# Sending a weight matrix's tail to chosen DMA engines through GpSimd's queue

## The chip, the cores and the metric

The kernel runs on one core of one Trainium2 chip. The metric is the time of one execution on the device in microseconds (us); lower is better. The page counts 16 DMA engines, and in the kernel before 16 packets are under way at 92 of 99 instants taken every 5 us (17 or 18 at the other seven). "The trace" is one profiled execution: every instruction, and for every DMA packet its start, its duration, its bytes and its queue. The trace does not say on which engine a packet ran. Engine numbers in this document are those that the marks of e3, e4 and e9 give; in the plan of the change they are what the author meant.

## The reference, cut to what matters

```python
x  = A_x                                    # 4 x 1 x 640, bf16
xn = layernorm(x)
# attention, 32 heads, head size 192, the last 2048 of 8192 cached keys
q  = xn @ wq
p  = softmax(q @ k.T * 192**-0.5)           # k, v: 2048 x 192 per head and batch
att = (p @ v) @ wo
# feed-forward: w1, w3 640 x 1536, w2 1536 x 640
ffn = (silu(xn @ w1) * (xn @ w3)) @ w2
out = x + att + ffn
```

Nearly all of the work is reading: 3 MB of K and 3 MB of V for each head, and the weights, 223 MB in all. w1 is under 2 MB of that.

## The kernel before: the parts that matter

Nearly all loads are issued by SyncE into one queue. A load of a tile of 128 partitions leaves 128 data packets in the trace, eight for each of the 16 engines, and 16 packets of 4 bytes, one for each engine. w1 has 640 rows of 1,536 numbers (3,072 bytes). 640 is five times 128, and the kernel splits it in three: 512 rows on all engines (four rows to a partition), 64 rows as 128 half rows on all engines, and 64 rows in small loads of 12 partitions (`w1_low`) on three engines alone. (The kernel before leaves 1,324 packets of 4 bytes on SyncE's queue. It has 82 loads of 128 partitions and four of 12, and 1,324 is 82 x 16 + 4 x 3.)

```python
LE, LI = 3, 4
LP, LF, LB = LE * LI, CT + LE * LI, KM * P + PH     # 12, 44, 576; CT = 32, KM = 4, PH = 64
FM, FH = KM * F, KM * F + F // 2

def w1_load():
    w = B_w1
    wt = fpool.tile([P, FH + F], BF16, tag="w", name="w1")
    we = wopool.tile([LF, 2 * F], BF16, tag="wo", name="w1e")
    nc.gpsimd.memset(we[:], 0.0)
    nc.gpsimd.memset(wt[0:LF, FH:], 0.0)
    nc.sync.dma_start(out=wt[:, 0:FM], in_=w[0:KM * P, :].rearrange("(p kc) n -> p (kc n)", kc=KM))
    nc.sync.dma_start(out=wt[:, FM:FH], in_=w[KM * P:LB, :].rearrange("r (h n) -> (r h) n", h=2))   # the half rows
    ...

def w1_low(n):                                      # called four times, between the loads of the heads
    if n < 2:
        b0 = LB + n * 2 * LP
        nc.sync.dma_start(out=we[n * CT:n * CT + LP, :],
                          in_=w[b0:b0 + 2 * LP, :].rearrange("(i e s) n -> e i (s n)", e=LE, s=2))
    ...

def w3_load():
    wt = fpool.tile([P, KC, F], BF16, tag="w", name="w3")
    nc.sync.dma_start(out=wt[:].rearrange("p k n -> p (k n)"), in_=B_w3.rearrange("(p kc) n -> p (kc n)", kc=KC))
```

The rest of the kernel loads K and V head by head, multiplies and sums on VectorE and TensorE, and adds the products of w1, w3, w2 and wo where their data has arrived.

## Time and profile before

| | before |
|---|---|
| time | 525.76 us (525.65 to 525.87, 3 runs; 525.68 over 6 with the later ones) |
| span of the profiled run | 523.8 us |
| TensorE, VectorE busy | 69%, 65% |
| share of the 16 DMA engines' span taken by SyncE's packets | 99.2% |
| last DMA packet ends | 520.48 us |

From the page of the kernel before: busy times; the DMA rows, whose 40 places are equal slices of the span (busy tenths, then GB/s); then the queues with packets, megabytes and their share of 16 engines' span.

```profile
span 523.8 us, 4820 instructions
PE 361.8 (69%) x2336; PEld 75.9 (14%) x1643; DVE 340.9 (65%) x413; ACT 55.8 (11%) x176; POOL 5.6 (1%) x12
...
DMA  9999999999999999999999999999999999999996
GB/s 389 422 443 425 433 431 432 428 433 432 430 435 428 437 418 446 424 437 426 434 434 429 432 434 429 435 427 435 425 437 434 427 437 431 430 434 425 441 418 275
...
q1 hardware_dynamic: 11868, 222.96, 99.2%
q8 instruction: 15, 0.25, 0.2%
```

The DMA engines are busy nine tenths or more in 39 of the 40 slices and the compute engines are not. So the kernel ends when the slowest of the 16 engines has moved its share. Queue 8 is the fetching of the program itself, 15 packets of 16 KB; it runs on the same engines (a SyncE packet of 24,576 bytes beside such a fetch takes 1.3 to 1.5 us instead of 0.91).

The end of the chain of waits of the kernel before (start, length, what):

```profile
465.17 24.49 DMA vt<-in_A_v_cache_dram
...
489.68 30.66 DMA w<-in_B_w_dram
...
520.38 0.76 PE acc L264 x8
521.13 0.47 DVE res L542
```

After the last landing only about 3.4 us follow. Two stretches of the run will be compared later. Here they are for the kernel before; the columns are the window, its length, the busy time and count of PE, PEld, DVE, ACT and POOL, TensorE's granted clock, the DMA share and GB/s.

```profile
26.00:39.00 13.00, 9.03 (x31) 0.30 (x3) 8.46 (x10) 1.56 (x3) 0.00 (x0) 0.74 0.99 425
39.00:53.00 14.00, 8.12 (x37) 0.80 (x8) 12.57 (x15) 2.19 (x5) 0.00 (x0) 0.98 1.01 432
53.00:66.00 13.00, 11.11 (x69) 2.00 (x45) 10.46 (x12) 1.39 (x5) 0.00 (x0) 0.89 1.02 436
```

GpSimd's clear of the tail's tile, and two issues on SyncE's queue, from the timelines of the kernel before (start, length, engine, line, operation):

```profile
9.07 2.65 POOL L390 MEMSET w1e<- 44x3072 bf16 x1
```

```profile
65.95 0.55 SPq L132 DMA_DIRECT2D vt<-in_A_v_cache_dram  x1
82.18 0.34 SPq L439 DMA_DIRECT2D w<-in_B_w_dram  x1
```

### The profile page before, as it was taken

The page shows a single profiled execution, that of the slowest core. Times are in us where ns is not written, and L with a number is a line of the kernel's source. Part 1 is how long each engine was busy: PE and PEld are TensorE (multiplying, and loading weights), DVE is VectorE, ACT ScalarE, POOL GpSimd, SP SyncE. Part 2 cuts the span into 40 slices and gives each one's busy share as a digit, 9 for nine tenths or more (in the row PEclk, how much of TensorE's full clock was granted, in tenths as well). Part 3 has the DMA queues.
Part 4 walks back from the last instruction along what each step waited for, and adds up shares of the span by engine and source line. Part 5 has one row for each costly group of instructions (what it writes and reads, how often), then busy time and mean ns, then how long its engine had stood idle before and what let it go on. Part 6 is the DMA issues. An engine that isn't in the chain of part 4 may idle for free.

```text
span 523.8 us, 4820 instructions
## 1 busy us (share of the span) xinstructions
PE 361.8 (69%) x2336; PEld 75.9 (14%) x1643; DVE 340.9 (65%) x413; ACT 55.8 (11%) x176; POOL 5.6 (1%) x12
## 2 busy tenths in 40 slices
PE   0965866887668776667547768586686876675685
PEld 0100111121111111111111111111111111111122
DVE  3268853687656767577646877466667766667671
ACT  2111111111001110101100111001101110011111
POOL 4000000000000000000000000000000000000000
PEclk9979886898878998789997988889878898889988
DMA  9999999999999999999999999999999999999996
GB/s 389 422 443 425 433 431 432 428 433 432 430 435 428 437 418 446 424 437 426 434 434 429 432 434 429 435 427 435 425 437 434 427 437 431 430 434 425 441 418 275
DMA packets 11904, 223.26 MB, mean 426 GB/s; under 512 B 1332, under 2 KB 1608, under 8 KB 3052
## 3 DMA queue, kind: packets, MB, share of 16 engines
q1 hardware_dynamic: 11868, 222.96, 99.2%
q8 instruction: 15, 0.25, 0.2%
q14 instruction: 5, 0.04, 0.0%
q10 hardware_dynamic: 16, 0.01, 0.0%
HBM read 222.96 MB, written 0.01 MB: 426 GB/s over the span
## 4 chain that ended last, share of the span: by engine, by line
DMA 60%; PE 20%; DVE 15%; ACT 3%; issue 1%; SPq 1%
DMA kt<-in_A_k_cache_dram 44%; PE ps L288 11%; DMA w<-in_B_w_dram 11%; DVE pr L277 10%; DMA vt<-in_A_v_cache_dram 5%; PE po L361 4%; PE qps L243 3%; DVE sc L296 2%; ACT ex L324 1%; DVE z L332 1%; DMA x_sb<-in_A_x_dram 1%; PE mt L318 1%; ACT L324 0%; ACT negm L321 0%; PE mt L305 0%
## 5 line engine op out<-in xcount | busy, mean ns | idle before, releaser
L288 PE MATMUL ps<-pr,idb 128*128 128x512 bf16 x768 | 214.7, 422 | 137.6 <-DVE pr L277 137.5
L277 DVE TENSOR_TENSOR pr<-kt,qbc 128x3072 bf16<-128x3072 bf16 x128 | 223.5, 1746 | 104.0 <-DMA kt<-in_A_k_cache_dram 104.0
L296 DVE TENSOR_REDUCE sc<-ps 128x16 f32<-128x512 f32 x128 | 87.1, 681 | 2.7 <-PE ps L288 2.6
L340 PE MATMUL o_ps<-vt,z 128*8 128x384 bf16 x1024 | 60.5, 380 | 0.2 <-DVE z L332 0.2
L361 PE MATMUL po<-o_sb,sel_w 128*32 128x192 f32 x128 | 49.2, 518 | 0.6 <-ACT o_sb L343 0.6
L340 PEld LDWEIGHTS <-z 128*8 128x8 bf16 x1024 | 26.2, 95 | 98.8 <-issue 89.2
L332 DVE TENSOR_TENSOR z<-ex,mask_b 128x256 bf16<-128x256 bf16 x32 | 13.5, 423 | 38.6 <-ACT ex L324 38.6
L343 ACT COPY o_sb<-o_ps 128x384 f32<-128x384 f32 x32 | 15.3, 478 | 196.9 <-PE o_ps L340 196.9
L313 ACT ACTIVATE gneg<-gmax 1x128 f32<-1x128 f32 x32 | 9.8, 308 | 162.8 <-DVE gmax L310 162.8
L305 PEld LDWEIGHTS mt<-idf,lmax 128*1 128x1 f32 x32 | 3.2, 101 | 127.5 <-issue 125.5
L361 PEld LDWEIGHTS po<-o_sb,sel_w 128*32 128x32 f32 x128 | 13.8, 130 | 29.4 <-issue 27.9
L288 PEld LDWEIGHTS <-idb 128*128 128x128 bf16 x124 | 12.0, 97 | 39.3 <-issue 32.8
L318 PEld LDWEIGHTS mt<-ones_ff,gneg 1*128 1x128 f32 x64 | 9.6, 186 | 47.1 <-issue 43.7
L243 PE MATMUL qps<-wt,xnT 128*128 128x512 bf16 x59 | 14.9, 412 | 0.1
L318 PE MATMUL mt<-ones_ff,gneg 1*128 1x1 f32 x64 | 12.3, 259 | 0.7 <-ACT gneg L313 0.7
L321 ACT COPY negm<-mt 128x1 f32<-128x1 f32 x32 | 5.1, 159 | 70.4 <-PE mt L318 70.4
L310 DVE TENSOR_REDUCE gmax<-mt 1x4 f32<-1x128 f32 x32 | 8.8, 274 | 5.8 <-PE mt L305 5.8
L348 PEld LDWEIGHTS po<-rsum,tot_w 128*32 128x32 f32 x64 | 4.4, 108 | 51.5 <-ACT ex L324 35.4
L249 DVE CAST qbc<-qps 128x512 bf16<-128x512 f32 x6 | 3.8, 684 | 11.7 <-PE qps L243 11.7
L324 ACT ACTIVATE ex<-sc,negm 128x64 bf16<-128x64 f32 x32 | 11.1, 348 | 1.0
L305 PE MATMUL mt<-idf,lmax 128*1 128x128 f32 x32 | 10.9, 340 | 0.0
L199 PE MATMUL xnT_ps<-idb,xn 4*128 4x4 bf16 x5 | 0.4, 178 | 13.4 <-DVE xn L194 13.4
(74 smaller groups left out, 84.4 us busy)
## 6 DMA issues: line engine op xcount, KB each, us to landing
kt<-in_A_k_cache_dram SPq DMA_DIRECT2D x32, 3072.0 KB, 19.1
vt<-in_A_v_cache_dram SPq DMA_DIRECT2D x32, 3072.0 KB, 25.5
wo_t<-in_A_wo_dram SPq DMA_DIRECT2D x8, 960.0 KB, 20.7
wt<-in_A_wq_dram SPq DMA_DIRECT2D x2, 3072.0 KB
w<-in_B_w_dram SPq DMA_DIRECT2D x1, 1920.0 KB
wt<-in_A_wq_dram SPq DMA_DIRECT2D x1, 1536.0 KB, 19.5
w<-in_B_w_dram SPq DMA_DIRECT2D x1, 1536.0 KB
w<-in_B_w_dram SPq DMA_DIRECT2D x2, 640.0 KB
```

The source lines that it names most:

```text
L243: nc.tensor.matmul(qp[:], lhsT=xnT[:, kc].rearrange("p a b -> p (a b)"), rhs=wq_rows[kc][:, (c0 + i) * QC:(c0 + i + 1) * QC], start=(kc == ...
L277: nc.vector.tensor_tensor(out=pr[:], in0=kts[h][:, g * JQ:(g + 1) * JQ, :], in1=qbc[:, h * Dh:(h + 1) * Dh].unsqueeze(1).to_broadcast([P, ...
L288: nc.tensor.matmul(ps[:], lhsT=idb[:], rhs=pr[:, :, kk * DD:(kk + 1) * DD], start=(kk == 0), stop=(kk == NK - 1))
L296: nc.vector.tensor_reduce(out=scs[h][:, g * JQ:(g + 1) * JQ], in_=pss.pop(u)[:], axis=AX.X, op=ALU.add)
L305: nc.tensor.transpose(out=mt[0:1, 0:P], in_=chs[h][0][:], identity=idf[:])
L313: nc.scalar.activation(out=gneg[:], in_=gmax[:].unsqueeze(1).to_broadcast([1, PB, B]), func=ACTF.Copy, scale=-SCALE)
L318: nc.tensor.matmul(mt[:, P:P + 1], lhsT=gneg[:].rearrange("o p b -> o (p b)"), rhs=ones_ff[:], start=True, stop=True)
L324: nc.scalar.activation(out=ex[:], in_=scs.pop(h)[:], func=ACTF.Exp, bias=negm[:, 0:1], scale=SCALE, accum_out=rsum[:])
L332: nc.vector.tensor_tensor(out=z[:], in0=ex[:].unsqueeze(2).to_broadcast([P, NJ, B]), in1=mask_b[:].unsqueeze(1).to_broadcast([P, NJ, B]), ...
L340: nc.tensor.matmul(o_ps[c * CT:c * CT + 2 * B, :], lhsT=z[:, 2 * jj:2 * jj + 2, :], rhs=vt[:, 2 * jj:2 * jj + 2, :], start=(jj < 4), stop= ...
L343: nc.scalar.copy(out=o_sb[:], in_=o_ps[:])
L361: nc.tensor.matmul(po[sl, 0:Dh], lhsT=sel_w[:, par].rearrange("p a b -> p (a b)"), rhs=o_sb[:, par * Dh:(par + 1) * Dh].rearrange("p (r i) ...
```

## The change

Its intent is balance. The 64 rows that travelled as half rows over all 16 engines are to ride on engines that finish early. The place from which GpSimd's queue starts its next load is called the cursor here. That it starts where its last load ended was the author's assumption when the prediction was made; the loads of the tail show it later (by the marks on engines 0 and 1, then 2 and 3 in e4; on 4 and 5, then 7 and 8 in e9). So 24 rows go to one pair of engines and 40 to another, and three tiny loads into unused tiles (`skip`) stand between, to move the cursor by 4, 1 and 7. The widths 4, 2, 1, 2, 7 add up to 16; as planned, the pairs would be engines 4 and 5, and 7 and 8. The tail of w1 moves into one buffer of the value pool, w3 is loaded in two pieces, and eight more small matmuls take the tail.

24 rows go to partitions 16 to 23, 40 rows to partitions 60 to 67.

The diff, cut to its core (the operands of the tail are rebuilt to the new row order, which is left out, as are the matmuls and the new places of the small SyncE loads of `w1_low`):

```diff
-    KM, PH, LE, LI = KC - 1, P // 2, 3, 4
-    LP, LF, LB = LE * LI, CT + LE * LI, KM * P + PH
+    KM, LE, LI, SA, SB, GP = KC - 1, 3, 4, 3, 5, 8
+    LP, LF, LB = LE * LI, 68, KM * P
+    PA, PZ = 16, LF - GP
+    RA = LB + 5 * LP + LI
+    RB = RA + SA * GP
 ...
+    def skip(k):
+        t = const.tile([k, CT], BF16, name=f"skip{k}")
+        n = CT if k > 1 else CT - 1
+        nc.gpsimd.dma_start(out=t[:, 0:n], in_=B_w1[0:k, 0:n])
 
     def w1_load():
-        wt = fpool.tile([P, FH + F], BF16, tag="w", name="w1")
-        we = wopool.tile([LF, 2 * F], BF16, tag="wo", name="w1e")
-        nc.gpsimd.memset(we[:], 0.0)
-        nc.gpsimd.memset(wt[0:LF, FH:], 0.0)
-        nc.sync.dma_start(out=wt[:, 0:FM], in_=w[0:KM * P, :].rearrange("(p kc) n -> p (kc n)", kc=KM))
-        nc.sync.dma_start(out=wt[:, FM:FH], in_=w[KM * P:LB, :].rearrange("r (h n) -> (r h) n", h=2))
+        wt = fpool.tile([P, KM * F], BF16, tag="w", name="w1")
+        we = vpool.tile([P, SB, F], BF16, tag="vt", name="w1e")
+        nc.gpsimd.memset(we[0:LF], 0.0)
+        nc.sync.dma_start(out=wt[:], in_=B_w1[0:KM * P, :].rearrange("(p kc) n -> p (kc n)", kc=KM))
+        for k, r0, p0, n in ((4, RA, PA, SA), (1, RB, PZ, SB)):
+            skip(k)
+            nc.gpsimd.dma_start(out=we[p0:p0 + GP, 0:n, :].rearrange("p s n -> p (s n)"),
+                                in_=B_w1[r0:r0 + n * GP, :].rearrange("(i e s) n -> e i (s n)", e=2, s=n))
+        skip(7)
 ...
     def w3_load():
-        nc.sync.dma_start(out=wt[:].rearrange("p k n -> p (k n)"), in_=B_w3.rearrange("(p kc) n -> p (kc n)", kc=KC))
+        for k0, k1 in ((0, KC - 2), (KC - 2, KC)):
+            nc.sync.dma_start(out=wt[:, k0:k1, :].rearrange("p k n -> p (k n)"),
+                              in_=B_w3.rearrange("(p kc) n -> p kc n", kc=KC)[:, k0:k1, :].rearrange("p k n -> p (k n)"))
```

More of the change, by code (lines that the diff above doesn't have):

```diff
@@ L201 @@
     nc.vector.tensor_copy(out=xnT[:], in_=xnT_ps[:].unsqueeze(2).to_broadcast([P, KC, PB, B]))
-    KM, PH, LE, LI = KC - 1, P // 2, 3, 4
-    LP, LF, LB = LE * LI, CT + LE * LI, KM * P + PH
-    assert D - LB == 5 * LP + LI and F % LE == 0
-    xm = ppool.tile([B, 2, PH, 2], BF16, tag="pr", name="xm")
-    nc.gpsimd.memset(xm[:], 0.0)
-    for i in range(2):
-        nc.vector.tensor_copy(out=xm[:, i, :, i], in_=xn[:, KM * P:LB])
-    xe = ppool.tile([B, 3 + LE, LF], BF16, tag="pr", name="xe")
+    KM, LE, LI, SA, SB, GP = KC - 1, 3, 4, 3, 5, 8
[3 more added lines that the diff above has]
+    RB = RA + SA * GP
+    assert RB + SB * GP == D and F % LE == 0
+    xe = ppool.tile([B, SB + LE, LF], BF16, tag="pr", name="xe")
     nc.gpsimd.memset(xe[:], 0.0)
@@ L221 @@
     for e in range(LE):
-        nc.vector.tensor_copy(out=xe[:, 3 + e, CT + e * LI:CT + (e + 1) * LI], in_=xn[:, LB + 5 * LP:D])
-    NX = KM + 2
-    xw_ps = ps_t.tile([P, NX + 3 + LE, B], BF16, tag="t", name="xw_ps")
+        nc.vector.tensor_copy(out=xe[:, SB + e, CT + e * LI:CT + (e + 1) * LI], in_=xn[:, LB + 5 * LP:RA])
+    for r0, p0, n in ((RA, PA, SA), (RB, PZ, SB)):
+        nc.vector.tensor_copy(out=xe[:, 0:n, p0:p0 + GP].rearrange("b s (e i) -> b s e i", e=2),
+                              in_=xn[:, r0:r0 + n * GP].rearrange("b (i e s) -> b s e i", e=2, s=n))
+    xw_ps = ps_t.tile([P, KM + SB + LE, B], BF16, tag="t", name="xw_ps")
     for kc in range(KM):
         nc.tensor.transpose(out=xw_ps[:, kc, :], in_=xn[:, kc:KM * P:KM], identity=idb[0:B, 0:B])
-    for i in range(2):
-        nc.tensor.transpose(out=xw_ps[:, KM + i, :], in_=xm[:, i].rearrange("b r h -> b (r h)"), identity=idb[0:B, 0:B])
-    for i in range(3 + LE):
-        nc.tensor.transpose(out=xw_ps[0:LF, NX + i, :], in_=xe[:, i, :], identity=idb[0:B, 0:B])
-    xw = const.tile([P, NX, NREP, B], BF16, name="xw")
-    nc.vector.tensor_copy(out=xw[:], in_=xw_ps[:, 0:NX, :].unsqueeze(2).to_broadcast([P, NX, NREP, B]))
-    xl = const.tile([LF, 3 + LE, NREP, B], BF16, name="xl")
-    nc.vector.tensor_copy(out=xl[:], in_=xw_ps[0:LF, NX:, :].unsqueeze(2).to_broadcast([LF, 3 + LE, NREP, B]))
+    for i in range(SB + LE):
+        nc.tensor.transpose(out=xw_ps[0:LF, KM + i, :], in_=xe[:, i, :], identity=idb[0:B, 0:B])
+    xw = const.tile([P, KM, NREP, B], BF16, name="xw")
+    nc.vector.tensor_copy(out=xw[:], in_=xw_ps[:, 0:KM, :].unsqueeze(2).to_broadcast([P, KM, NREP, B]))
+    xl = const.tile([LF, SB + LE, NREP, B], BF16, name="xl")
+    nc.vector.tensor_copy(out=xl[:], in_=xw_ps[0:LF, KM:, :].unsqueeze(2).to_broadcast([LF, SB + LE, NREP, B]))
     qbc = const.tile([P, H * Dh], BF16, name="qbc")
@@ L382 @@
     ffn = {}
-    FM, FH = KM * F, KM * F + F // 2
+    def skip(k):
+        t = const.tile([k, CT], BF16, name=f"skip{k}")
+        n = CT if k > 1 else CT - 1
+        nc.gpsimd.dma_start(out=t[:, 0:n], in_=B_w1[0:k, 0:n])
     def w1_load():
-        w = B_w1
-        wt = fpool.tile([P, FH + F], BF16, tag="w", name="w1")
-        we = wopool.tile([LF, 2 * F], BF16, tag="wo", name="w1e")
-        nc.gpsimd.memset(we[:], 0.0)
-        nc.gpsimd.memset(wt[0:LF, FH:], 0.0)
-        nc.sync.dma_start(out=wt[:, 0:FM], in_=w[0:KM * P, :].rearrange("(p kc) n -> p (kc n)", kc=KM))
-        nc.sync.dma_start(out=wt[:, FM:FH], in_=w[KM * P:LB, :].rearrange("r (h n) -> (r h) n", h=2))
-        ffn["w1"], ffn["w1e"] = wt, we
+        wt = fpool.tile([P, KM * F], BF16, tag="w", name="w1")
+        we = vpool.tile([P, SB, F], BF16, tag="vt", name="w1e")
+        nc.gpsimd.memset(we[0:LF], 0.0)
+        nc.sync.dma_start(out=wt[:], in_=B_w1[0:KM * P, :].rearrange("(p kc) n -> p (kc n)", kc=KM))
+        ffn["w1"], ffn["w1e"] = wt, we
+        for k, r0, p0, n in ((4, RA, PA, SA), (1, RB, PZ, SB)):
[3 more added lines that the diff above has]
+        skip(7)
     def w1_low(n):
-        w, wt, we = B_w1, ffn["w1"], ffn["w1e"]
+        w, we = B_w1, ffn["w1e"]
         if n < 2:
             b0 = LB + n * 2 * LP
-            nc.sync.dma_start(out=we[n * CT:n * CT + LP, :],
+            nc.sync.dma_start(out=we[n * CT:n * CT + LP, 0:2, :].rearrange("p s n -> p (s n)"),
                               in_=w[b0:b0 + 2 * LP, :].rearrange("(i e s) n -> e i (s n)", e=LE, s=2))
         elif n == 2:
-            nc.sync.dma_start(out=wt[0:LP, FH:FH + F], in_=w[LB + 4 * LP:LB + 5 * LP, :].rearrange("(i e) n -> e i n", e=LE))
+            nc.sync.dma_start(out=we[0:LP, 2, :], in_=w[LB + 4 * LP:LB + 5 * LP, :].rearrange("(i e) n -> e i n", e=LE))
         else:
-            nc.sync.dma_start(out=wt[CT:LF, FH:FH + F // LE], in_=w[LB + 5 * LP:D, :].rearrange("i (e n) -> e i n", e=LE))
+            nc.sync.dma_start(out=we[CT:CT + LP, 2, 0:F // LE], in_=w[LB + 5 * LP:RA, :].rearrange("i (e n) -> e i n", e=LE))
     def w1_in():
@@ L419, in w1_in @@
         main(0)
-        for w in range(HG):
-            c0 = FM + (w % 2) * FW
-            mm(w, xw[:, KM + w // 2], wt[:, c0:c0 + FW])
-        for i in range(2):
+        for i in range(SB):
             for w in range(HG):
-                mm(w, xl[:, i], we[:, i * F + w * FW:i * F + (w + 1) * FW])
-        for w in range(HG):
-            mm(w, xl[:, 2], wt[0:LF, FH + w * FW:FH + (w + 1) * FW])
+                mm(w, xl[:, i], we[0:LF, i, w * FW:(w + 1) * FW])
         FE = F // LE
@@ L432, in w1_in @@
                 if c0 < c1:
-                    mm(w, xl[:, 3 + e], wt[0:LF, FH + c0 - e * FE:FH + c1 - e * FE], c0 - w * FW)
+                    mm(w, xl[:, SB + e], we[0:LF, 2, c0 - e * FE:c1 - e * FE], c0 - w * FW)
         for kc in range(1, KM):
```

## The prediction

> **What bounds it now.** The DMA engines. The page shows DMA at nine tenths or more in 39 of 40 slices, 426 GB/s, queue 1's packets filling 99.2% of 16 engines' span; PE (69%) and DVE (65%) are no limits. The chain of waits ends in two landings (24.5 us of a value tile, 30.7 us of w2); after the last (520.4 us) only 3.4 us follow. So the time is set by the slowest of the 16 engines.
>
> **Balance.** By the trace's packet records a packet costs about 8 ns plus its bytes at 27.2 B/ns (24,576 B 912 ns, 1,536 B 65 ns, 15,360 B 573 ns). Following packets back to back gives the ends of the engines: two at 517.24 us, one each near 517.5, 518.1 and 518.6, eleven at 519.6 to 520.49. The mean is about 519.4: perfect balance is worth 1.1 us. The early ones met few or no instruction fetches; a 16 KB fetch takes 0.93 us and stretches a neighbouring packet by 0.5, and 15 of those and 5 smaller ones fall in the span.
>
> **The change** moves 64 rows of w1 (128 half rows) from all 16 engines to four.
> - All engines: 8 packets of 65 ns and a semaphore write less, -0.50 us; w3 in two pieces, +0.05 us. [...] Net -0.40 us. No run shows this yet.
> - One pair gets 4 packets of 9,216 B each, +1.4 us (net +1.0); the other 4 of 15,360 B, +2.3 (net +1.9). [...] The trace names no engines; I infer that the pairs are among the five early ones. They then end at 519.0 to 519.6, still before the rest.
> - PE: 8 more small products, hidden. GpSimd: one clear of 68x7680 instead of 44x3072 and 44x1536; at 2.65 us per 3,072 columns an estimated 6.6 us, from about 29 us, done before SyncE writes there (42 us).
> - w1's tail takes a value buffer, so the value load issued at 66 us waits for a weighted sum (about 74). Its packets start only at 84.5 us: the queue should not run dry.
>
> **On the critical path:** only the -0.40 us of the eleven slow engines; their last end moves from 520.49 to about 520.1.
>
> **Prediction: 525.35 us** (before 525.76), 80% range 524.9 to 526.1. Faster by over 2%: 0.01; within 2%: 0.98; slower by over 2%: 0.01.
>
> **What would show it right.** DMA still at 9, no idle time of the engines near 80 to 90 us; the 1,536 B packets gone, 8 packets each of 9,216 and 15,360 B on a GpSimd queue, in two pairs of chains; last landing near 520.0, the ends closer together; otherwise the same chain of waits.
>
> **What would make it wrong.** GpSimd's queue spreads its 8 partitions over 8 engines instead of 2 (+0.9 us on each: near 526.2), or cuts rows into short packets; the pairs meet engines with two fetches (+1.9 us: 527.6); fetches fall on other engines because the programs differ; [...] the software queue adds work at start or end. A gain over 0.6 us would mean that the slow engines carried something else that the change removes.

Cut from the text above was a term of the sum: +0.05 us (5 x 9 ns) for the posts of GpSimd's five loads on all 16 engines. The terms left for all engines are −0.50 and +0.05, so −0.45; the "net −0.40", the "net +1.0" and "net +1.9" of the pairs, the last end of 520.1 and the forecast of 525.35 us still hold the cut term. (e2 later showed ten packets on each engine for five such loads, and a 4-byte packet takes 9 ns.)

## More of the kernel before

All timed runs with several rounds were in the fast state. Three experiments (e3, e4, e9) are single looks, so their state is unknown; only the placement of packets is read from them.

## The result, and the profile after

| | before | after |
|---|---|---|
| median of 6 runs | 525.68 us (525.63 to 525.87) | 530.21 us (529.86 to 530.94) |
| ratio, 95% interval | | 1.0088 (1.0075 to 1.0101) |
| span of the profiled run | 523.8 us | 528.1 us |
| packets of GpSimd's (software) queue | none | 256 |
| mean end of the 16 engines | 519.37 us | 522.08 us |
| last end | 520.48 us | 524.63 us |

A ratio here is the mean time of one kernel's fast runs over that of the other's of the same rounds, so not quite the ratio of the medians that are quoted. The kernel became 4.5 us slower, where 0.4 us less was predicted; it stays within 2%.

The same rows of the page of the changed kernel:

```profile
span 528.1 us, 4835 instructions
...
DMA  9999999999999999999999999999999999999995
GB/s 386 426 439 341 429 429 432 432 432 433 431 428 436 428 429 442 423 439 426 433 436 426 437 424 433 437 428 436 424 434 436 428 434 431 432 432 429 436 420 226
...
q1 hardware_dynamic: 11868, 222.76, 98.8%
...
q0 software_dynamic: 256, 0.20, 0.1%
```

Look at the fourth slice (39.6 to 52.8 us): 341 GB/s against 425 before, and yet the engines still read as busy nine tenths. They had packets under way the whole time, but the packets moved slowly. The three stretches of the changed kernel say the same:

```profile
26.00:39.00 13.00, 9.03 (x31) 0.30 (x3) 8.43 (x10) 1.56 (x3) 9.22 (x6) 0.77 0.98 423
39.00:53.00 14.00, 8.33 (x36) 0.80 (x8) 12.41 (x15) 2.19 (x5) 0.00 (x0) 0.97 1.02 355
53.00:66.00 13.00, 9.28 (x51) 1.66 (x39) 6.71 (x9) 0.79 (x2) 0.00 (x0) 0.65 1.00 429
```

In 39 to 53 us the DMA share is 1.02 in one and 1.01 in the other, and the rate is 355 against 432 GB/s: (432 − 355) × 14 us is about 1.08 MB not moved, which at 432 GB/s is 2.5 us for the whole core. Compute is the same in that window; only in the next one does it fall back (DVE 6.71 against 10.46 us), because its data came late. The shares above 1 show that such columns carry an error of a few per cent; the rate is the better witness.

The packet records say where those 2.5 us sit. In the kernel before, after the first few microseconds and except beside a fetch, a packet's duration depends on its size alone: 24,576 bytes take 912 ns, 12,288 take 460. Counting the SyncE packets between 38 and 56 us that took over 12 ns more than their usual time:

```
            stretched packets    sum of the excess over 16 engines
before              1                    0.03 us
after             169                    2.42 us
```

They are packets of K and w1 for all partitions, on all engines: 12,288 bytes took 476 to 960 ns, and 24,576 bytes 927 to 1,599. They stretch from 41.0 to 51.8 us; the packets of the two GpSimd loads run from 41.0 to 51.2. Those stretch too: of the eight of 9,216 bytes the first four still took the usual 347 or 348 ns, the others 393 to 555; those of 15,360 bytes took 704 to 785 instead of 573 (one of them, beside a fetch of the program, 1,387).

Following the packets back to back gives the end of each of the 16 engines, in order:

```
before: 517.23 517.23 517.49 518.11 518.55 519.59 519.70 520.00 520.11 520.17 520.19 520.21 520.21 520.25 520.40 520.48
after:  519.63 520.03 520.10 520.52 520.75 522.02 522.11 522.17 522.25 522.32 522.41 522.52 523.35 523.90 524.49 524.63
```

The last end moved by 4.15 us. Of this 2.70 is common to all: the mean moved from 519.37 to 522.08. The other 1.45 is unevenness: last minus mean grew from 1.11 to 2.56 us. Four engines stand late, and five are still early. So two things have to be explained: a loss on every engine, and a tail carried by the wrong engines.

The chain of waits of the changed kernel at the place where w1 is waited for:

```profile
41.79 17.58 DMA kt<-in_A_k_cache_dram
...
59.39 25.53 DMA w1e<-in_B_w_dram
...
84.96 2.43 PE f_ps L417 x22
```

GpSimd in the changed kernel, from its timeline:

```profile
28.86 6.49 POOL L392 MEMSET w1e<- 68x7680 bf16 x1 [26.52 <-PE qps L242]
35.31 0.66 POOL L387 DMA_DIRECT2D skip<-in_B_w_dram  x1
35.96 0.59 POOL L397 DMA_DIRECT2D w1e<-in_B_w_dram  x1
36.51 0.52 POOL L387 DMA_DIRECT2D skip<-in_B_w_dram  x1
37.02 0.58 POOL L397 DMA_DIRECT2D w1e<-in_B_w_dram  x1
37.57 0.52 POOL L387 DMA_DIRECT2D skip<-in_B_w_dram  x1
```

And SyncE's queue in the changed kernel:

```profile
42.42 0.87 SPq L405 DMA_DIRECT2D w1e<-in_B_w_dram  x1
...
74.41 0.54 SPq L132 DMA_DIRECT2D vt<-in_A_v_cache_dram  x1
87.43 0.81 SPq L440 DMA_DIRECT2D w<-in_B_w_dram  x2
```

The clear took 6.49 us (estimated: 6.6) and ended before SyncE's first load into the tile at 42.42 us. The value load came at 74.4 instead of 66.0 us, and w3's at 87.4 instead of 82.2; in neither place does the DMA row fall. The rows show no cost of these waits, and e5 and e8 below, which keep them, confirm that there is none to speak of.

### The profile page after: what moved, and what is told of

It is laid out like the page before. It is cut to its first block, busy times and chain, and to the rows that moved or that the text cites. A ratio compares the mean times of both kernels' runs of the same rounds, so it can differ in the third digit from the quotient of the medians.

```text
span 528.1 us, 4835 instructions
## 1 busy us (share of the span) xinstructions
PE 362.3 (69%) x2341; PEld 76.7 (15%) x1647; DVE 339.4 (64%) x413; ACT 55.8 (11%) x176; POOL 10.8 (2%) x15
## 4 chain that ended last, share of the span: by engine, by line
DMA 63%; PE 20%; DVE 13%; ACT 2%; issue 1%; SPq 0%
DMA kt<-in_A_k_cache_dram 47%; PE ps L287 11%; DVE pr L276 9%; DMA w<-in_B_w_dram 6%; DMA w1e<-in_B_w_dram 5%; DMA vt<-in_A_v_cache_dram 5%; PE po L360 4%; PE qps L242 3%; DVE sc L295 2%; ACT ex L323 1%; DMA x_sb<-in_A_x_dram 1%; DVE z L331 1%; PE mt L317 1%; PE o_ps L339 1%; PE f_ps L417 0%
## 5 line engine op out<-in xcount | busy, mean ns | idle before, releaser
L339 PE MATMUL o_ps<-vt,z 128*8 128x384 bf16 x1024 | 58.8, 372 | 0.2 <-DVE z L331 0.2
L263 PE MATMUL acc<-wo_t,oT 128*4 128x320 bf16 x96 | 9.2, 298 | 0.6 <-DMA wo_t<-in_A_wo_dram 0.6
```

The costliest lines, as they stand in the source:

```text
L339: nc.tensor.matmul(o_ps[c * CT:c * CT + 2 * B, :], lhsT=z[:, 2 * jj:2 * jj + 2, :], rhs=vt[:, 2 * jj:2 * jj + 2, :], start=(jj < 4), stop= ...
```

## The experiments

The first theory was about the route: that GpSimd's queue itself costs something that slows the other packets (the packets it puts on every engine, 256 in the changed kernel), and that the pairs may sit on other engines than meant. It is "theory S" in the expectations. Its rival, V, was that the value buffer, the later waits of SyncE or w3's two pieces make SyncE's queue run dry. Neither was right as put (e5 and e8 keep the value buffer, the waits and the pieces, and their engines end at a mean of 519.6 and 519.5 us, against 519.4 before), and after e1 a third one took over: **which engine writes which partitions**. By it, the loss common to all engines comes from the tail's partitions being written by the wrong engines, and goes when either is changed; it is "theory C" in the expectations. What the runs show is which pairings of engines and partitions stretched packets and which did not. All versions of the kernel below gave correct results.

| run | what it tries | median, us | ratio to before, 95% interval |
|---|---|---|---|
| after | the change | 530.21 | 1.0088 (1.0075 to 1.0101) |
| e1 | 64 rows by SyncE to 16 partitions in a row | 527.15 | 1.0028 (1.0011 to 1.0045) |
| e2 | before and five tiny GpSimd loads | 525.86 | 1.0009 (0.9994 to 1.0024) |
| e5 | pairs write partitions 0 to 15 | 527.58 | 1.0035 (1.0020 to 1.0050) |
| e6 | after without its three tiny loads | 529.88 | 1.0083 (1.0068 to 1.0098) |
| e7 | e1 with the 16 partitions spread | 526.41 | 1.0020 (1.0003 to 1.0036) |
| e8 | after with tiny loads that do move the cursor | 526.67 | 1.0019 (1.0004 to 1.0034) |
| e10 | an attempt to use only engines with room | 528.13 | 1.0044 (1.0030 to 1.0057) |
| e11 | all 64 rows on engines 7 and 8 | 526.44 | 1.0004 (0.9990 to 1.0018) |

The kernel before, run beside them on the same chips, had medians of 525.68 to 525.98 us. All changes keep within 2%; the intervals and the packets are what is read.

### e1_sync_load: the same rows without GpSimd's queue

```diff
-        for k, r0, p0, n in ((4, RA, PA, SA), (1, RB, PZ, SB)):
-            skip(k)
-            nc.gpsimd.dma_start(out=we[p0:p0 + GP, 0:n, :].rearrange("p s n -> p (s n)"),
-                                in_=B_w1[r0:r0 + n * GP, :].rearrange("(i e s) n -> e i (s n)", e=2, s=n))
-        skip(7)
+        nc.sync.dma_start(out=we[PA:PA + 16, 0:4, :].rearrange("p s n -> p (s n)"),
+                          in_=B_w1[RA:D, :].rearrange("(q s) n -> q (s n)", s=4))
```

> The changed kernel, but its 64 rows come in one DMA on SyncE's queue (16 partitions of 4 rows, one 12,288 B packet on each of 16 engines), with no GpSimd DMA; value buffer, w3 in two pieces and the products stay. Theory S (the software queue's packets hold up all 16 engines, 2.7 us of the 4.2 us by which the last landing moved, and its data lands on wrong engines, the other 1.5): all of the loss goes, 525.5 to 526.0 us, mean end of the engines near 519.4. Rival V (the value buffer, the later waits of SyncE or w3's pieces make the queue run dry): the loss stays, 529 us or more.

Measured: 527.15 us (526.91 to 527.67), 1.45 us over before. Neither number came out, and the reason is in the page of e1: the fourth slice sags here too, without any GpSimd load.

```profile
GB/s 390 423 444 377 441 428 427 432 434 428 431 434 432 434 423 437 431 432 434 431 431 430 436 426 434 434 430 434 423 434 436 430 432 432 431 436 428 434 418 272
```

37 SyncE packets are stretched, by 1.32 us summed over 16 engines; the mean end rises from 519.37 to about 520.64. So this much comes without GpSimd's queue. What e1 shares with the change is the destination: a few partitions in a row. Here 16 packets of 12,288 bytes, one on each engine, go into partitions 16 to 31 (SyncE's queue has 32 packets more than before, 16 of data and a 4-byte one for each engine).

### e2_five_tiny: the queue without the rows

```diff
 (kernel before, in w1_load)
+        for i in range(5):
+            t = const.tile([4, CT], BF16, name=f"tiny{i}")
+            nc.gpsimd.dma_start(out=t[:], in_=B_w1[0:4, 0:CT])
```

> The kernel before, with five GpSimd DMAs of 4 rows of 64 B into scratch added at w1's load; nothing reads them. Theory S with a cost for every packet (0.17 us each; 2 packets on each engine for such a DMA, 10 in all): the engines' mean end moves by 1.5 to 1.9 us, time near 527.4. Theory S with a cost for every DMA (5 DMAs as in the change): 2.7 us, time near 528.4. Rival V: nothing, 525.7 to 526.

Measured: 525.86 us (525.75 to 527.24), within 0.2 us of before by the medians. The five loads made 160 packets on the software queue: ten on each engine. In the changed kernel there were 256, sixteen on each: 12 from the tiny loads (62 or 64 bytes), 16 from the tail and 228 of 4 bytes. The counts fit if for each load every engine gets as many packets as the busiest one, those without data being 4 bytes long, and one more of 4 bytes, taken to be the semaphore post ((1+1)+(4+1)+(1+1)+(4+1)+(1+1) = 16). None of this costs the 1.5 to 2.7 us of theory S, nor does it stretch other packets: none was stretched in the time when the tiny loads ran (17 to 24 us). The profiled run is the one of 527.24; in it one engine ended at 522.02, the next at 520.63. Its two fetches (at 58.8 and 310.4 us) are no more than most engines meet; it had fallen behind before 92 us. In this run 23 SyncE packets were stretched between 45 and 56 us, by 0.18 us summed over 16 engines, though no tail and no tiny load ran then; why stays open. The mean end was 519.70, so 0.3 us of mean end is what a single profile may show without the tail's loads.

### e3_before_marked and e4_after_marked: giving the engines names

```diff
+    def mark(k):
+        t = const.tile([k, 64 + 2 * k], BF16, name=f"mark{k}")
+        n = 64 + 2 * k if k > 1 else 61
+        nc.sync.dma_start(out=t[:, 0:n], in_=B_w1[0:k, 0:n])
+
+    for i, k in enumerate((1, 2, *range(4, 16))):
+        add(40 + 8 * (i // 2), 1, mark, k)
```

Fourteen SyncE loads of 1 to 15 partitions, each with its own packet size, stamp every chain of packets (in the trace each left as many packets as it has partitions). The marks give the engines their numbers: the chain that has all the sizes is called engine 0, the one that lacks only the first is engine 1, and so on. There is no load of three, so engines 2 and 3 are told apart by the 12-partition loads: in e3 three chains are late by them (135.30 to 136.07 us in the table below), and the next, at 133.92, is called 3.

> The kernel before, with 14 tiny SyncE loads of 1 to 15 partitions spread over its middle[...], so that each chain of packets can be given its engine's number. Time within 0.5 us of before. Theory P (the pairs of the change were meant for 4-5 and 7-8): these are four of the five engines that end early (517.2 to 518.6 us). Rival: the early ones are others.

> The changed kernel with the same markers. If the cursor stood at 0, engines 4-5 and 7-8 are later than their neighbours by 1.4 and 2.3 us from 55 us on. What the trace of the change suggests instead: two of engines 0-2 late by 1.4 us more than the common delay of 2.1, and the third and one other by 2.3 us, that is pairs 0-1 and 2-3 or a like place. Time near 530 us.

Measured, as single runs: 525.98 and 530.33 us; the marks cost about 0.1 to 0.3 us. When the first packet of the second load of wo ran on each engine shows how late each of them was:

```
engine            0       1       2       3       4       5       7       8       9      15
e3 (before)    135.45  136.07  135.30  133.92  132.79  132.81  132.88  132.87  132.80  133.23
e4 (after)     138.58  139.19  140.11  138.69  135.29  135.04  136.06  136.00  135.10  135.03
later by         3.1     3.1     4.8     4.8     2.5     2.2     3.2     3.1     2.3     1.8
```

Every engine is later by about 2 us. Engines 0 to 3 are later by more, in two pairs, so the 24 rows run on 0 and 1, and the 40 rows on 2 and 3: not on 4 and 5, nor on 7 and 8. Engines 7 and 8 are later by more as well (3.2 and 3.1 us), though they carry no row of the tail. They are the two that the 40 rows were meant for; why they are late is not shown. (Engines 4 and 5, meant for the 24 rows, hardly show it: 2.5 and 2.2 us.) Engines 0 to 3 were never early: in the kernel before 0, 1 and 2 already carry the 12-partition loads, and 3 meets three of the five smaller fetches of the program. Nor was the intended place quite right: in e3 engines 4, 7 and 8 are among the five early ones, as expected, but engine 5 is not; it meets two fetches and ends at about 520.0.

### e5_own_ports: the same engines, other partitions

```diff
-    LP, LF, LB = LE * LI, 68, KM * P
-    PA, PZ = 16, LF - GP
+    LP, LF, LB = LE * LI, 44, KM * P
+    PA, PZ, NB = 0, 8, 5            # the pairs' rows to partitions 0 to 7 and 8 to 15, in other columns
```

> The changed kernel with the same five GpSimd DMAs, but the pairs' rows written to partitions 0-7 and 8-15 (slices 3 to 7 of a taller tail)[...]; in the change they are written to partitions 16-23 and 60-67[...]. Theory C[...]: the stretching of packets between 39 and 54 us goes, the engines' mean end falls from 522.1 to 519.4-519.9; engines 0-3 stay late by what they carry, the last at 521.5 to 522.3: time 526.8 to 527.6. Theory S (the software queue as such costs every engine): mean end stays near 522, time 530.

Measured: 527.58 us (527.43 to 527.69), so 2.6 us of the 4.5 us are gone. The sag is gone too. The page and the stretch of 39 to 53 us of e5:

```profile
GB/s 384 426 441 425 431 429 426 431 435 430 428 438 428 431 429 437 429 436 426 432 431 432 436 423 438 430 433 430 430 432 434 430 434 431 430 433 432 434 417 226
```

```profile
39.00:53.00 14.00, 8.25 (x34) 0.80 (x8) 11.30 (x13) 2.19 (x5) 1.90 (x4) 0.93 1.03 436
```

425 GB/s in the fourth slice, 436 in the stretch; two stretched packets (0.06 us) instead of 169; every packet of the tail at its usual 347 or 573 ns. The bytes, the queue and the tiny loads are those of the change, and so, by the same order of loads, should be the engines; what differs is the partitions written. With them the clear grew to 10.3 us, so that the pairs' packets ran from 42.8 us instead of 41.0; e8, where they ran from 42.0, is the check on that. This is the run that shows theory C for the common loss: from these engines, the rows to partitions 0 to 15 stretch packets by 0.06 us, those to 16 to 23 and 60 to 67 by 2.42. The rest, some 1.9 us over before, is the unevenness: mean end 519.6, last 522.21, and a late group behind it at 521.7 and 521.3, which are the engines that carry the pairs.

### e6_no_skips: do the tiny loads move anything?

```diff
-            skip(k)
 ...
-        skip(7)
```

> The changed kernel without its three tiny loads, two GpSimd DMAs left. If the tiny loads don't move the cursor, the pairs still land on 0-1 and 2-3 and the time stays at 529.5 to 530.5. If they do move it, the pairs move and the lateness of engines 0-3 changes. Theory S with a cost for each packet: 10 packets on each engine instead of 16, a third of the common 2.7 us less, 529.3.

Measured: 529.88 us (529.69 to 530.79) against 530.21: the same. The software queue falls to 160 packets, the stretching stays (148 packets, 2.20 us), the mean and last ends are 521.78 and 524.46 us. The tiny loads of the change move no cursor. Why they do not is not shown; they differ from the loads of the tail, which do move it (e4), in the form of their source, and e8 changes that.

### e7_sync_spread: e1 with the partitions spread

```diff
-        nc.sync.dma_start(out=we[PA:PA + 16, 0:4, :].rearrange("p s n -> p (s n)"),
+        nc.sync.dma_start(out=we[0:64:4, 3:7, :].rearrange("p s n -> p (s n)"),
```

> The SyncE version of the 64 rows (e1), but the 16 partitions 4 apart, 0 to 60[...]. Theory C: of e1's 1.4 us, most goes: 525.8 to 526.3 us, and packets right after are stretched by less than half as much. Rival (the value buffer, the later waits, w3's pieces): as e1, 527.1.

Measured: 526.41 us (526.11 to 527.41); mean end about 519.77, last 520.84; 21 stretched packets, 0.38 us, 20 of them between 45 and 47 us, right where the tail runs. The time is a little above what was expected. The same rows by the same queue in packets of the same 12,288 bytes, but now each four partitions in a row take one packet instead of four: 12,288 bytes instead of 49,152. The loss in mean end shrinks from 1.27 to 0.40 us, which a theory of "rows cost more than their bytes" would not give.

### e8_cursor_moved: the change as it was meant

```diff
-        t = const.tile([k, CT], BF16, name=f"skip{k}")
-        n = CT if k > 1 else CT - 1
-        nc.gpsimd.dma_start(out=t[:, 0:n], in_=B_w1[0:k, 0:n])
+        t = const.tile([2 * k, CT], BF16, name=f"skip{k}_{len(skips)}")
+        skips.append(t)
+        nc.gpsimd.dma_start(out=t[:], in_=B_w1[0:2 * k, 0:CT].rearrange("(i e) n -> e i n", e=k))
 ...
-        for k, r0, p0, n in ((4, RA, PA, SA), (1, RB, PZ, SB)):
-            skip(k)
+        for ks, r0, p0, n in (((4,), RA, PA, SA), ((7, 10), RB, PZ, SB)):
+            for k in ks:
+                skip(k)
```

The source now has two levels, as the loads of the tail have. 7 + 10 stands for the 1 of the change, if the cursor goes round the 16 engines (the marks of e9 fit this: 4 + 2 + 7 + 10 is 23, and the second pair runs on 7 and 8), because a source of one share would have no second level.

> The changed kernel with its tiny loads reshaped to have the same form as the pairs' loads (two-level source, 2k partitions in k groups: k = 4 before the first pair, 7 and 10 before the second, 7 after), so that the cursor should stand at 4 and at 7. Theory C: the pairs land on engines 4-5 and 7-8[...]; no packet is stretched, engines 0-3 are no longer late: what was predicted for the change, 525.2 to 525.7 us. Theory S: 19 packets on each engine, 530 us or more.

Measured: 526.67 us (526.29 to 527.15), 3.5 us better than the change; still 0.19% (0.04 to 0.34) over before, and 1 us over the top of what was expected. The page and the stretch of e8:

```profile
GB/s 390 420 444 421 430 434 426 432 436 426 433 435 431 436 423 435 427 438 427 433 435 428 431 436 433 429 432 427 432 432 438 426 436 428 431 435 428 436 417 250
```

```profile
39.00:53.00 14.00, 7.84 (x35) 0.80 (x8) 12.62 (x14) 2.19 (x5) 0.26 (x1) 1.00 1.01 430
```

One stretched packet; the tail's packets all at 347 and 573 ns; the partitions written are those of the change. So the partitions were not wrong in themselves: it was the wrong engines that wrote them (0 to 3 by e4, where by the marks of e9 it is now 4, 5, 7 and 8). The mean end is 519.53 us and fifteen engines end by 520.17. One ends at 521.32, and it sets the time.

### e9_cursor_marked: who is the late one?

This is e8 with the marks of e3.

> The kernel with the moved cursor (e8) with the 14 markers. Theory: the one engine that still ended late there (521.3 us, the next 520.2) is engine 4, which carries two fetches in the kernel before as well and so had no room for 12 more rows; engines 5, 7 and 8, which have room, end by 520. Rival: another engine, 9 or above, because the data landed elsewhere.

Measured: 527.12 us, once. The wo packets now come at 134.90, 135.78 and 135.25 us on engines 0, 1 and 2, at 133.94 and 134.03 on 4 and 5, at 134.96 and 134.74 on 7 and 8, and at 132.90 on 15: the tail is on 4 and 5 and on 7 and 8, as meant. The late engine is 5, not 4 as expected, with an end at 521.44 us. The marks also show where the program's fetches fall. In this run the 16 KB ones go round engines 5, 6, 9, 10, 11, 12, 13 and 14, and each costs its engine 1.42 us (0.93 for itself and about 0.5 of stretch in a neighbour). Engine 5 got two, at 179 and 445 us. Engines 0, 2, 7, 8 and 15 met none. In e3 engines 7, 8 and 15 end at 517.4 to 517.6, and those that meet two fetches at about 520, engine 5 among them: it never had room for 12 rows of the tail. Which of the eight meets which fetch is not fixed: in e3 engine 5 met those at 212 and 475 us.

### e10_room_only: a miss

```diff
+        nc.gpsimd.dma_start(out=we[PZ:PZ + GP, 0:NB, :].rearrange("p s n -> p (s n)"),
+                            in_=B_w1[RB:D, :].rearrange("(i e s) n -> e i (s n)", e=2, s=NB))
+        skip(6)
+        nc.gpsimd.dma_start(out=we[PA:PA + 4, 0:6, :].rearrange("p s n -> p (s n)"),
+                            in_=B_w1[RA:RB, :].rearrange("(a b) n -> a (b n)", a=3))
```

It was to put 40 rows on 7 and 8, and 24 rows on engine 15 alone (partitions 92 to 95), by a source of three parts that was meant to keep the load to one engine.

> As e8, but data only on engines with room: 40 rows on 7-8 as there; the other 24 rows in one DMA meant for engine 15 alone (cursor moved by 6 more[...]). Theory: last landing at 519.9 to 520.3, time 525.1 to 525.6, 0.1 to 0.5 us under before. If 15 isn't the engine that takes it or has no room, one engine ends 2 us late, 527 or more.

Measured: 528.13 us (527.82 to 528.63), far from what was expected. The load of the 24 rows left four packets of 18,432 bytes, and four engines instead of one wrote them into four partitions in a row. (The software queue has 176 packets, eleven on each engine. By the count of e2, four packets on one engine would have made it 14 and 224.) They took 687 to 2,099 ns, where about 686 would be usual by the prediction's rule (8 ns and 27.2 bytes per ns), and the fourth slice sags again:

```profile
GB/s 389 422 441 356 435 425 434 430 437 426 430 440 422 439 425 434 430 432 434 432 430 435 430 433 434 430 431 430 427 435 434 431 434 429 435 430 435 432 419 274
```

42 SyncE packets are stretched, by 1.9 us over 16 engines; the mean end is about 521.50. As a design it failed, but it gives the loss a third dose.

### e11_one_pair: all 64 rows where there is room

```diff
-    KM, LE, LI, SA, SB, GP = KC - 1, 3, 4, 3, 5, 8
+    KM, LE, LI, SA, SB, GP = KC - 1, 3, 4, 0, 8, 8
 ...
-        for ks, r0, p0, n in (((4,), RA, PA, SA), ((7, 10), RB, PZ, SB)):
+        for ks, r0, p0, n in (((7,), RB, PZ, SB),):
```

(The diff is against e8.)

> The moved cursor (e8) without its first pair: all 64 rows go to engines 7-8, 32 rows each, partitions 60 to 67, three GpSimd DMAs left. In e8 one engine ended at 521.3 us, 1.2 later than the engine with the same fetch (375.6 us) in the kernel before; if that is an engine of the first pair that had no room for 12 more rows, it now ends near 520 like the others with two fetches, and 7 and 8 are at 520.3 to 520.7 (517.2 - 0.4 + 3.7): time 525.4 to 526.0, against 526.7 for e8. If the late engine is not of that pair, it stays: 526.5 or more.

Measured: 526.44 us (525.72 to 527.13), ratio 1.0004 (0.9990 to 1.0018): the same as before (525.4 to 526.0 was expected). One stretched packet (0.03 us), the tail's packets at the usual 912 ns. The late engine of e8 is gone, which shows that it was one of the first pair. Following the packets, the two engines that carry the rows (7 and 8, if the cursor stood where e9 shows it) end at 520.52 and 520.79, now the last, and those that meet fetches by 520.17. Time varied more (before: 525.49 to 527.29), so tenths can't be read from it. No version beat the kernel before.

### The dose

In three runs several engines write partitions that lie close together, with different amounts. The third column counts the bytes into the fullest four partitions in a row (four, as an engine of a pair carries four packets); the last two are what was measured, the mean end of the 16 engines against 519.37:

```
run   the load                                     bytes into four partitions   stretch    mean end later by
e7    16 packets of 12,288, partitions 4 apart               12,288             0.38 us       0.40 us
e1    16 packets of 12,288, partitions 16 to 31              49,152             1.32 us       1.27 us
e10   4 packets of 18,432, partitions 92 to 95               73,728             1.9 us        2.13 us
```

The moved bytes themselves change the mean end by little: the half rows go and the same 64 rows come. The loss grows with the bytes into neighbouring partitions. (The 0.40 of e7 is hardly more than the 0.3 us that e2 shows without such a load; e1 and e10 are clear of that.) An estimate found after the runs comes near e1 and e10: the time of those bytes at 27.2 bytes per ns (the rate of a single packet in the kernel before), less that of one packet. It is 1.81 − 0.45 = 1.36 us for e1 and 2.71 − 0.68 = 2.03 us for e10; for e7 it is nothing. For the change the same sum gives, for 36,864 bytes in four partitions of the first pair, 1.36 − 0.35 = 1.0 us, and after it for 61,440 bytes of the second, 2.26 − 0.57 = 1.7 us; together 2.7 us, where 2.42 us of stretch and +2.70 of mean were measured. It is a sum that fits and no mechanism, and bytes are not all of it: e8 puts the same bytes into the same partitions by other engines, and its mean end is later by 0.16 us only. The first pair's packets did end when the second's began (44.9 us). Of the stretch 0.62 us fell before that moment and 1.80 after, so the estimate is good for the second pair and too high for the first.

## Why the prediction was wrong

It said 525.35 us with a range of 524.9 to 526.1; 530.21 us was measured. What failed are one step and one missing term.

- **The step that failed:** "The trace names no engines; I infer that the pairs are among the five early ones." It rested on the assumption that the tiny loads move a cursor. The tiny loads don't move it (e6: 529.88 us without them), and the pairs sit on engines 0 to 3 (e4), which were not early. This is the 1.45 us of unevenness. The risk was listed ("the pairs meet engines with two fetches (+1.9 us: 527.6)"), but as a matter of fetches, and the range did not hold even that.
- **The term that the sum lacked:** where the bytes land. The prediction costed packets as if a packet's time depended on its size alone, and looked for the effect in the engines' own work. Engines 0 to 3 wrote partitions 16 to 23 and 60 to 67, and packets on all 16 engines were stretched: +2.70 us on the mean, where the prediction had −0.40 for eleven engines. e5 takes this away by changing the partitions, e8 by changing the engines; e1 and e10, and less clearly e7, show it grow with the bytes into neighbouring partitions.
- **Even done as meant, it gains nothing.** e8 removes both faults and still loses 0.2%, since engine 5 meets two fetches and has no room (e9): the inference of the pairs' place was wrong for engine 5 even with the cursor moved. With all rows on 7 and 8 (e11) it comes out even. "Perfect balance is worth 1.1 us" was a bound and not a forecast. That the 16 KB fetches fall on eight engines (5, 6 and 9 to 14 in e9), but not each on the same one in every version (engine 5's came at 179 and 445 us in e9, at 212 and 475 in e3), was not known.
- **Right:** the DMA engines bound the kernel, before and after. The packets are 8 each of 9,216 and 15,360 bytes, and the packets of 1,536 bytes are gone. The packets that GpSimd's loads put on all engines are cheap (e2: ten on each, +0.2 us at the medians for five loads). The clear took 6.49 us for 6.6 estimated and did not delay SyncE. The late value load and w3's pieces did not run the queue dry. The eight small matmuls are hidden.
- **Right in part:** the saving of 0.40 us on the engines that carry no tail shows once the two faults are gone: in e11 they end by 520.17 us, against 520.48 before. "Otherwise the same chain of waits" holds at its end, 4.2 us later, but in 41 to 85 us the chain goes through K and the w1 tail.

What stays open: why packets are held up on all 16 engines when a few write the wrong partitions. The stretched packets show the size (169 of them, 2.42 us), and no run shows the mechanism. Nor is it shown which engines suit which partitions beyond those tried, or whether the estimate under "The dose" holds outside of the sizes tried.

## What to carry to other kernels

When the DMA engines were the limit here, an uneven load had two prices: the engine that carries it (1.45 us of unevenness), and which engine writes which partitions (2.70 us of mean end). The second went when the same engines wrote other partitions (e5, 2 stretched packets instead of 169) or other engines wrote the same partitions (e8, 1): so try a small load at other partitions, and count the stretched packets. Look at GB/s, not at the busy share, to see whether packets run at their usual speed (341 GB/s in the changed kernel's fourth slice, where the DMA row reads 9). A balance worth 1 us needs to know which engine carries which bytes, the program's own fetches included (1.42 us each in e9): stamp the engines with small marked loads before moving anything.
